# Loading query and key tiles singly instead of in neighbour-token groups, with more transposes by DMA, a new order and a longer warm-up

## The chip, the cores and the metric

The kernel runs on one core of a Trainium2 chip. The metric is the device time of one execution in microseconds, the median of three runs. The profiled span of the program, from its first to its last instruction, is a little shorter than that time.

## The reference, cut to what matters

Attention with a sliding window of 96 tokens and 8 global tokens, with a bias that falls with distance, is followed by an FFN that takes the elementwise maximum of three products (maxout) and multiplies it with an output matrix.

```python
batch, n_heads, seq, head_dim = (4, 8, 768, 64)       # q, k, v: float32
n_global, n_local = (8, 96)
n_tokens, d_model, d_ff = (3072, 512, 768)

def _attn_ref(q, k, v, n_global, n_local):
    scores = scale * np.matmul(q, k.transpose(0, 1, 3, 2))
    rel = pos[:, None] - pos[None, :]
    is_global = pos[None, :] < n_global
    is_local = (rel >= 0) & (rel < n_local)
    keep = is_global | is_local
    dist = np.where(is_global & ~is_local, float(n_local), np.abs(rel))
    slopes = 2.0 ** (-8.0 * (np.arange(H) + 1) / H)
    scores = np.where(keep, scores - slopes * dist, -1e9)   # shapes cut
    a = softmax(scores)                                     # written out in the original
    return np.matmul(a, v)

def _moe_ref(x, w1, w2, w3, w_out):
    h = np.maximum(np.maximum(x @ w1, x @ w2), x @ w3)
    return h @ w_out

# x is the attention's output with the heads side by side: (4 * 768, 512)
```

## The kernel before

The 3072 tokens are 24 tiles of 128. A tile attends to itself and the tile before it in its batch (six tiles a batch); the 8 global keys and values are copied over the first 8 rows of the tile before. Seven chunks of 4, 2, 2, 4, 4, 4 and 4 tiles then go through the FFN. Every step is a unit of a few instructions, and a string, `SCHEDULE`, says in which order the units are put into the program; each engine executes its own instructions in that order. A unit's last number often chooses the engine (0 ACT, 1 DVE, 2 POOL).

| unit | what it does |
|---|---|
| `l n.s` | load a part of a group of neighbouring tokens, q or k (L158) |
| `L T` | load q and k of tile T |
| `v T`, `w g.j`, `o i` | load v of tile T (L174), a part of w1, w2 or w3 (L417), a part of w_out |
| `c`, `C T.0`, `C T.1`, `W`, `Q` | cast a group's part, q and k of a tile, v of a tile, weights, w_out to bf16 |
| `x n.s`, `X T` | transpose q and k so that the head's 64 numbers lie in partitions |
| `S T.g` | scores of four heads and their exponential |
| `M T.g` | multiply by the mask with its bias (when the bias wasn't put in by matmul) |
| `A T` | attention times v, and division by the sum |
| `T T` | transpose the result for the FFN (xT) |
| `F c.f.j` | FFN: 128 columns of w1, w2 or w3 (j) for chunk c, and the maximum |
| `O c.t` | product with w_out of one tile, and its store; `E` is the last chunk's |
| `G`, `V` | global keys and values; `K`, `B` make mask and bias; `D` matmuls of zeros |

A group puts `e` neighbouring tokens of a head in one partition, so that a contiguous piece in memory is e × 256 bytes:

```python
GROUPS = [[0, 2], [2, 2], [4, 2], [6, 4], [10, 2]]       # first tile, tiles in the group
raw_pool  = ctx.enter_context(tc.tile_pool(name="raw", bufs=6))
rawv_pool = ctx.enter_context(tc.tile_pool(name="rawv", bufs=6))
stage_pool = ctx.enter_context(tc.tile_pool(name="stage", bufs=3))
psS = ...(bufs=1, PSUM)   # tags sp0 and sp1: scores, and attention's output
psH = ...(bufs=3, PSUM)   # FFN, output, some transposes
psT = ...(bufs=1, PSUM)   # transposes

def load_part(n, s):      # l: 512 KB in one DMA
    bb, t0, sz, a, j0, jn = part(n, s)
    ...
    src = (q, k)[a][bb, 2 * j0:2 * (j0 + jn), t0 * 128:(t0 + sz) * 128, :]
    nc.sync.dma_start(out=r, in_=src.rearrange("h (i e) d -> i h (e d)", e=sz))

def load(T):              # L: 256 KB for q, 256 KB for k
    ...
    for i, src in enumerate((q, k)):
        nc.sync.dma_start(out=r[:, i], in_=src[b, :, sl, :].rearrange("h s d -> s h d"))

def u_x(n, s, how):       # x: 8 transposes on TensorE, then copies to qkT on ACT, DVE or both
    ...
            for e in range(sz):
                for j in range(lo, hi):
                    nc.tensor.transpose(tp[:, e, j - lo], ..., identb)          # L239
    for (lo, hi, pool, tag, copy), tp in zip(halves, tps):
        copy(dst[:, lo:hi], tp.rearrange("c e j i -> c j i e"))                 # L243

def u_X(T, how):          # X: by DMA (how 4), or 8 transposes on TensorE
    ...
    if how == 4:
        nc.sync.dma_start_transpose(out=qk..., in_=qb[T]...)                    # L250
        return
    ...
    for a in range(2):
        for jp in range(NP):
            nc.tensor.transpose(tps[a][:, jp], qb[T][:, a, jp * 128:(jp + 1) * 128], identb)

def u_XT(T, how):         # T: by DMA (how 4, L340), or 4 transposes on TensorE
    ...
    for jp in range(NP):
        nc.tensor.transpose(tp[:, jp], x[:, jp * 128:(jp + 1) * 128], identb)   # L349
    copies[how](xT[c][:, :, i * 128:(i + 1) * 128], tp)

def u_F1(c, f, j):        # F
    ps = psH.tile([128, W], FP32, name="h", tag="h")
    for dm in range(4):
        nc.tensor.matmul(ps, w123[f // 2][:, dm, j, ...], xT[c][:, dm], ...)    # L361
    if j == 0:   nc.scalar.copy(h01, ps)                                        # L366
    elif j == 1: nc.vector.tensor_max(h01s[c, f], h01s[c, f], ps)               # L368
    else:        nc.vector.tensor_max(ht[c][:, f], h01s[c, f], ps)              # L370

def u_D(i, n):
    wp = psH.tile([128, 512], FP32, name="wp", tag="h")
    for _ in range(n):
        nc.tensor.matmul(wp, zeros[:, 0:128], zeros, start=True, stop=True)     # L436
```

`cast` can also split a tile between DVE (q) and POOL (k) when its last number is 3. All DMAs but one go through SyncE's queue, in the order of the program: one that waits for its data or its buffer holds up those behind it.

Of the kernel before, what the change touches and what calls it, by code (L numbers as in the profile page):

```python
# [22 lines left out]


SCHEDULE = """
    K0 K1 K2 K3 K4 K5 l1.0 l1.1 D0.3 c0.0.2 B0.1 B1.1 B2.1 B3.0 K6 B4.1 B5.1 c0.1.1 c1.0.2 x0.0.4 B6.1
    B7.1 x0.1.4 S0.0.1 v0 l2.0 l2.1 K7 S0.1.1 G0.0 S1.0.1 S1.1.0 x1.0.3 c1.1.2 M0.0 M0.1 M1.0 v1 x1.1.4
    C0.1.2 v2 A0.1 G1.2 S2.0.1 M1.1 c2.0.2 x2.0.1 C1.1.1 S2.1.0 G2.2 S3.0.1 M2.0 M2.1 C2.1.1 T0.1 S3.1.1
    M3.0 M3.1 c2.1.2 v3 A1.0 C3.1.0 w0.0 V1.2 x2.1.2 w1.0 A2.1 V2.2 A3.0 T1.0 T2.1 T3.1 W1.0.1 W0.0.0
    G3.2 S4.0.0 S4.1.0 F0.0.0 F0.1.0 M4.0 F0.2.0 F0.3.0 G4.1 S5.0.0 M4.1 S5.1.0 w0.1 W0.1.1 w0.2 W0.2.2  # L30
    V3.2 F0.0.1 F0.1.1 F0.0.2 F0.1.2 v4 C4.1.0 A4.0 V4.2 w1.1 W1.1.2 W2.0.0 F0.4.0 F0.5.0 M5.0 M5.1 w1.2
    W1.2.2 v5 W2.1.0 T4.0 F0.2.1 F0.3.1 l3.0 l3.2 F0.4.1 l3.1 c3.0.2 c3.2.2 F0.5.1 o2 C5.1.0 A5.1 l3.3
    F0.2.2 Q2.2 F0.3.2 W2.2.0 o0 T5.0 F0.4.2 o1 F0.5.2 x3.0.0 F1.0.0 F1.1.0 c3.1.1 F1.2.0 x3.2.0 Q0.2
    F1.0.1 F1.1.1 F1.2.1 l4.0 l4.1 c3.3.0 F1.0.2 F1.1.2 F1.2.2 x3.1.2 x3.3.1 F1.3.0 F1.4.0 Q1.2 F1.3.1
    S6.0.0 S6.1.0 v6 v7 v8 G6.0 F1.3.2 F1.5.0 v9 c4.0.1 F1.4.1 S7.0.0 S7.1.0 G7.2 v10 M6.0 M6.1 M7.0
    M7.1 O0.0.0 F1.4.2 c4.1.1 C6.1.2 C7.1.2 L12 F1.5.1 S8.0.0 S8.1.0 x4.0.0 O0.1.0 A6.0 x4.1.2 A7.1 V7.2
    F1.5.2 v11 T6.0 O0.2.0 T7.1 G8.2 C8.1.2 S9.0.0 S9.1.0 G9.1 v12 v13 O0.3.0 F2.0.0 F2.1.0 S10.0.0 M8.0
    M8.1 M9.0 M9.1 S10.1.0 C9.1.2 L13 L14 F2.0.1 F2.1.1 F2.0.2 A8.0 C12.0.1 F2.1.2 G10.2 O1.0.0 V8.2
    A9.1 X12.1 M10.0 M10.1 C10.1.0 C11.1.0 F2.2.0 S11.0.0 S11.1.0 M11.0 M11.1 L15 F2.3.0 F2.4.0 O1.1.0
    V9.2 A10.1 F2.2.1 V10.2 T8.0 F2.3.1 F2.5.0 T9.0 A11.1 F2.4.1 T10.0 F2.2.2 F2.3.2 T11.1 F2.4.2  # L40
    S12.0.0 S12.1.0 F2.5.1 C13.0.2 C14.0.2 C15.0.1 X13.4 F3.0.0 F3.1.0 F3.0.1 G12.1 C12.1.0 F3.2.0
    F3.1.1 F3.2.1 S13.0.0 S13.1.0 F2.5.2 v14 C13.1.0 C14.1.2 M12.0 M12.1 F3.0.2 F3.1.2 X14.4 F3.2.2
    X15.4 G13.2 M13.0 M13.1 S14.0.0 S14.1.0 F3.3.0 F3.4.0 F3.5.0 M14.0 M14.1 G14.1 A12.0 A13.1 F3.3.1
    F3.4.1 F3.5.1 S15.0.0 M15.0 S15.1.0 G15.0 v15 V13.2 L16 L17 v16 T12.4 v17 M15.1 O2.0.0 C15.1.0 A14.0
    V14.2 F3.3.2 F3.4.2 T13.4 F3.5.2 C16.1.0 C16.0.2 X16.3 T14.4 C17.0.2 A15.1 X17.4 O2.1.0 S16.0.0
    S16.1.0 G16.1 L18 V15.2 L19 T15.1 M16.0 O3.0.0 M16.1 F4.0.0 F4.1.0 F4.0.1 F4.1.1 C18.0.2 L20 C19.0.2
    A16.1 F4.2.0 F4.3.0 S17.0.0 S17.1.0 F4.2.1 F4.0.2 F4.3.1 v18 M17.0 v19 M17.1 X18.3 X19.4 C20.0.0
    V16.2 F4.1.2 C17.1.2 O3.1.1 A17.1 F4.2.2 F4.3.2 S18.0.0 M18.0 S18.1.0 M18.1 F4.4.0 T16.4 T17.4
    F4.4.1 C18.1.2 C19.1.1 F4.4.2 X20.4 G18.1 S19.0.0 S19.1.0 F4.5.0 L21 M19.0 M19.1 v20 F4.5.1 A18.0
    T18.4 F4.5.2 A19.1 T19.4 V19.1 C21.0.1 X21.4 G19.1 L22 C22.0.2 L23 X22.4 O3.2.1 O3.3.0 O4.0.1  # L50
    S20.0.0 S20.1.0 M20.0 G20.0 O4.1.0 F5.0.0 F5.1.0 F5.2.0 S21.0.0 S21.1.0 G21.2 F5.0.1 F5.1.1 M20.1
    M21.0 F5.3.0 F5.0.2 F5.1.2 F5.2.1 F5.2.2 v21 C20.1.1 C21.1.2 F5.4.0 S22.0.0 M21.1 S22.1.0 C23.0.0
    F5.3.1 M22.0 M22.1 F5.5.0 F5.3.2 A20.0 V20.2 G22.2 v22 F5.4.1 X23.4 v23 F5.5.1 T20.4 A21.1 V21.1
    T21.4 F5.4.2 F5.5.2 S23.0.0 S23.1.0 M23.0 O4.2.0 M23.1 C22.1.2 A22.0 C23.1.0 O4.3.0 V22.2 T22.4
    A23.1 T23.4 O5.0.1 O5.1.0 O5.2.1 O5.3.0 F6.0.0 F6.1.0 F6.0.1 F6.0.2 F6.2.0 F6.3.0 F6.4.0 F6.1.1
    F6.2.1 F6.1.2 F6.3.1 F6.4.1 F6.2.2 F6.3.2 F6.5.0 F6.4.2 F6.5.1 F6.5.2 E
"""


# [1 line left out]
def kernel(  # L61
# [13 lines left out]
    nc = tc.nc  # L75
# [12 lines left out]
    slopes = [2.0 ** (-8.0 * (h + 1) / H) for h in range(H)]  # L88
    sizes = [4, 2, 2, 4, 4, 4, 4]

    GROUPS = [[0, 2], [2, 2], [4, 2], [6, 4], [10, 2]]
    assert sum(sizes) == NTT
    chunks, where = [], {}
    for n in sizes:
# [27 lines left out]
    zeros = persist.tile([128, 512], BF16, name="zeros")  # L122
# [21 lines left out]
    def part(n, s):  # L144

        T0, sz = GROUPS[n]
        jn = {2: 4, 4: 2, 6: 1}[sz]
# [3 lines left out]
    def load_part(n, s):  # L151

        bb, t0, sz, a, j0, jn = part(n, s)
        r = raw_pool.tile([128, 2 * DM], FP32, name="rawp", tag="raw")
        r = r[:, 0:sz * jn * 128].rearrange("i (h x) -> i h x", h=2 * jn)
        raw["p", n, s] = r
        src = (q, k)[a][bb, 2 * j0:2 * (j0 + jn), t0 * 128:(t0 + sz) * 128, :]
        nc.sync.dma_start(out=r, in_=src.rearrange("h (i e) d -> i h (e d)", e=sz))  # L158
# [273 lines left out]
    def u_D(i, n):  # L432

        wp = psH.tile([128, 512], FP32, name="wp", tag="h")
        for _ in range(n):
            nc.tensor.matmul(wp, zeros[:, 0:128], zeros, start=True, stop=True)  # L436

    with tc.manual_schedule():
        load_part(0, 0)
        load_part(0, {2: 1, 4: 2, 6: 4}[GROUPS[0][1]])  # L440

# [68 lines left out]
```

The softmax here doesn't subtract the row's maximum and nothing guards it: scores larger than these inputs give would overflow.

## Time and profile before

The median is 180.43 us (180.39 to 180.48 in three runs).

| what | before |
|---|---|
| profiled span | 178.5 us |
| FFN matmuls, line L361 | 99.2 us busy |
| output matmuls, L376 | 33.1 us busy |
| score matmuls, L283 | 352 of them |
| transposes of groups, L239 | 96 of them, 8.5 us busy |
| transposes of xT, L349 | 52 of them, 4.9 us busy |
| transposes by DMA | 9 of q and k (median 3.3 us to landing), 11 of xT (2.4 us) |
| DMA packets | 83587, of which 66160 under 512 B |

In a page of the profile, the first part gives each engine's busy time, its share of the span and its instructions; PE is TensorE, PEld its weight loads, which run beside the matmuls. The second part cuts the span into 40 slices of 4.5 us; a digit is the busy share in tenths. The chain is followed back from the last instruction to what released each step. Line numbers are those of the kernel before and are marked in the code above. `tpp` is a group's transposed q or k in PSUM, `tp` that of a single tile, `xtp` the transposed result of attention, `sp` scores, `op` attention's output, `h` the FFN's.

### The profile page before, as it was taken

The page shows a single profiled execution, that of the slowest core. Times are in us where ns is not written, and L with a number is a line of the kernel's source. Part 1 is how long each engine was busy: PE and PEld are TensorE (multiplying, and loading weights), DVE is VectorE, ACT ScalarE, POOL GpSimd, SP SyncE. Part 2 cuts the span into 40 slices and gives each one's busy share as a digit, 9 for nine tenths or more (in the row PEclk, how much of TensorE's full clock was granted, in tenths as well). Part 3 has the DMA queues.
Part 4 walks back from the last instruction along what each step waited for, and adds up shares of the span by engine and source line. Part 5 has one row for each costly group of instructions (what it writes and reads, how often), then busy time and mean ns, then how long its engine had stood idle before and what let it go on. Part 6 is the DMA issues. An engine that isn't in the chain of part 4 may idle for free.

```text
span 178.5 us, 3963 instructions
## 1 busy us (share of the span) xinstructions
PE 167.1 (94%) x1529; PEld 95.9 (54%) x1551; DVE 119.1 (67%) x237; ACT 103.2 (58%) x160; POOL 37.4 (21%) x65
## 2 busy tenths in 40 slices
PE   3599799999999999999999999999999999999991
PEld 0455645458866677845555555454454555444451
DVE  4519975977796689748978448978358986137610
ACT  4867898646689958555753936351862543440131
POOL 4255203543343012210006024100020401000000
PEclk9999999999999999999999999999999999999998
DMA  5999999999998899899544999988989664700015
GB/s 139 292 270 243 357 321 383 319 361 356 252 194 229 218 254 227 142 204 234 92 90 122 167 253 231 145 172 152 182 156 300 123 129 147 252 12 4 0 47 190
DMA packets 83587, 35.52 MB, mean 199 GB/s; under 512 B 66160, under 2 KB 78320, under 8 KB 83568
## 3 DMA queue, kind: packets, MB, share of 16 engines
q1 hardware_dynamic: 83424, 35.20, 83.6%
q8 instruction: 12, 0.20, 0.5%
q10 hardware_dynamic: 144, 0.07, 0.1%
q14 instruction: 7, 0.06, 0.1%
HBM read 25.17 MB, written 6.29 MB: 176 GB/s over the span
## 4 chain that ended last, share of the span: by engine, by line
PE 88%; ACT 3%; DVE 2%; POOL 2%; issue 1%; DMA 1%; POOLq 0%; ACTq 0%
PE h L361 53%; PE po L376 16%; PE sp L283 7%; PE op L322 3%; PE op L325 3%; PE tpp L239 3%; PE xtp L349 2%; ACT wmask L300 2%; PE sp L275 2%; DMA out_dram<-ost 1%; DVE qkT L243 1%; DVE xb L332 1%; ACT ost L382 1%; ACT P L288 1%; PE tp L261 1%
## 5 line engine op out<-in xcount | busy, mean ns | idle before, releaser
L361 PE MATMUL h<-xT,w 128*128 128x512 bf16 (+1 forms) x491 | 99.2, 348 | 0.7 <-issue 0.2
L361 PEld LDWEIGHTS <-w 128*128 128x128 bf16 x504 | 47.0, 98 | 40.4 <-ACT w L427 0.2
L288 ACT ACTIVATE P<-sp 128x1024 bf16<-128x1024 f32 (+1 forms) x48 | 43.4, 954 | 20.4 <-PE sp L283 20.2
L368 DVE TENSOR_TENSOR h<-h,h 128x512 bf16<-128x512 bf16 (+1 forms) x42 | 25.2, 609 | 25.6 <-PE h L361 15.5
L366 ACT CAST h<-h 128x512 bf16<-128x512 f32 (+1 forms) x42 | 21.6, 532 | 21.5 <-PE h L361 21.3
L376 PE MATMUL po<-wo,ht 128*128 128x512 bf16 (+2 forms) x147 | 33.1, 362 | 0.5
L370 DVE TENSOR_TENSOR ht<-h,h 128x512 bf16<-128x512 bf16 (+1 forms) x42 | 25.0, 606 | 3.7 <-PE h L361 3.0
L307 DVE TENSOR_TENSOR P<-P,wmask 128x1024 bf16<-128x1024 bf16 x36 | 24.8, 716 | 3.6 <-ACT P L288 3.5
L382 ACT COPY ost<-po 128x512 f32<-128x512 f32 (+2 forms) x20 | 11.2, 564 | 18.4 <-PE po L376 11.2
L376 PEld LDWEIGHTS <-ht 128*128 128x128 bf16 x156 | 14.0, 98 | 13.8
L332 DVE TENSOR_TENSOR xb<-op,rz 128x512 bf16<-128x512 f32 x24 | 16.6, 691 | 0.8
L283 PEld LDWEIGHTS <-qkT 64*128 64x128 bf16 x352 | 10.2, 96 | 10.0 <-issue 8.0
L283 PE MATMUL sp<-qkT 64*128 64x128 bf16 x352 | 15.2, 223 | 0.4 <-DVE xb L332 0.4
L322 PEld LDWEIGHTS <-P 128*128 128x128 bf16 x192 | 12.5, 97 | 2.7 <-ACT P L288 0.2
L221 POOL COPY va<-vaf 8x260 int32<-8x260 int32 x14 | 6.3, 449 | 34.7 <-PE op L325 34.7
L198 POOL CAST qkb<-raw 128x1024 bf16<-128x1024 f32 x7 | 7.2, 1037 | 27.6 <-DMA raw<-in_k_dram 27.6
L322 PE MATMUL op<-va,P 128*128 128x65 bf16 x160 | 12.4, 193 | 0.3 <-ACT va L189 0.2
L239 PE MATMUL tpp<-identb,qkp 128*128 128x128 bf16 x96 | 8.5, 246 | 4.0 <-POOL qkp L183 3.5
L325 PEld LDWEIGHTS <-P 128*128 128x128 bf16 x160 | 10.4, 97 | 1.8 <-issue 0.2
L239 PEld LDWEIGHTS <-qkp 128*128 128x128 bf16 x96 | 7.0, 112 | 5.8 <-POOL qkp L183 4.4
L325 PE MATMUL op<-va,P 128*128 128x65 bf16 x128 | 9.9, 193 | 0.1
L243 ACT COPY qkT<-tpp 128x1024 bf16<-128x1024 bf16 (+1 forms) x9 | 7.9, 873 | 3.4 <-PE tpp L239 3.4
(66 smaller groups left out, 107.7 us busy)
## 6 DMA issues: line engine op xcount, KB each, us to landing
rawv<-in_v_dram SPq DMA_DIRECT2D x24, 256.0 KB, 4.9
out_dram<-ost SPq DMA_DIRECT2D x23, 256.0 KB, 2.3
rawp<-in_q_dram SPq DMA_DIRECT2D x6, 512.0 KB, 7.3
rawp<-in_k_dram SPq DMA_DIRECT2D x6, 512.0 KB, 7.7
wst<-in_moe_w_dram SPq DMA_DIRECT2D x3, 1024.0 KB, 10.3
raw<-in_q_dram SPq DMA_DIRECT2D x12, 256.0 KB, 4.2
raw<-in_k_dram SPq DMA_DIRECT2D x12, 256.0 KB, 4.7
wst<-in_moe_w_dram SPq DMA_DIRECT2D x3, 512.0 KB, 8.6
```

The costliest lines, as they stand in the source:

```text
L239: nc.tensor.transpose(tp[:, e, j - lo], qb["p", n, s][:, e, 2 * j:2 * j + 2].rearrange("i h d -> i (h d)"), identb)
L283: nc.tensor.matmul(sp[:, hh, j2, ds], qT(T - ds, 1)[hsl, jp], qT(T, 0)[hsl, jp], start=not how, stop=True, skip_group_check=True)
L288: nc.scalar.activation(P[:, :, 0:n], sp.rearrange("p a b d n -> p (a b) d n")[:, :, 0:n], AF.Exp, bias=0.0, scale=scale)
L307: nc.vector.tensor_mul(P, P, wmask[:, g, :, 0:2])
L322: nc.tensor.matmul(o, P[:, i, 0], heads(va[T])[:, h], start=True, stop=(t == 0), skip_group_check=True)
L325: nc.tensor.matmul(o, P[:, i, 1], heads(va[T - 1])[:, h], start=False, stop=True, skip_group_check=True)
L332: nc.vector.tensor_tensor(out=x.rearrange("p (g h) d -> p g h d", g=2), in0=o4[:, :, :, 0:64], in1=rz[:, :, :, None].to_broadcast([128, 2, ...
L361: nc.tensor.matmul(ps, w123[f // 2][:, dm, j, (f % 2) * 128:(f % 2) * 128 + 128], xT[c][:, dm], start=(dm == 0), stop=(dm == 3))
L366: nc.scalar.copy(h01, ps)
L368: nc.vector.tensor_max(h01s[c, f], h01s[c, f], ps)
L370: nc.vector.tensor_max(ht[c][:, f], h01s[c, f], ps)
L376: nc.tensor.matmul(po, ht[c][:, f, tt * 128:(tt + 1) * 128], wo[:, f, cols], start=(f == 0), stop=(f == NF - 1))
```

## The change

Only the tiles 0 to 3 are still loaded as groups of neighbouring tokens. The tiles 4 to 23 are loaded singly, in pieces of 256 bytes. Of these 20 tiles 13 are transposed by DMA, seven by TensorE; 14 of the 24 results of attention are transposed by DMA. The matmuls of zeros are shorter (128 columns in place of 512), and 54 of them in place of 3 stand at the start, so as to keep TensorE active until data comes; three more stand further on. The order of all units is new, and many casts and copies go to other engines: 10 instead of 5 of the outputs are copied by DVE, 9 instead of 4 of the values cast by DVE.

```diff
 SCHEDULE = """
-    K0 K1 K2 K3 K4 K5 l1.0 l1.1 D0.3 c0.0.2 B0.1 B1.1 B2.1 B3.0 K6 B4.1 B5.1 c0.1.1 c1.0.2 x0.0.4 B6.1
-    B7.1 x0.1.4 S0.0.1 v0 l2.0 l2.1 K7 S0.1.1 G0.0 S1.0.1 S1.1.0 x1.0.3 c1.1.2 M0.0 M0.1 M1.0 v1 x1.1.4
-    C0.1.2 v2 A0.1 G1.2 S2.0.1 M1.1 c2.0.2 x2.0.1 C1.1.1 S2.1.0 G2.2 S3.0.1 M2.0 M2.1 C2.1.1 T0.1 S3.1.1
-    M3.0 M3.1 c2.1.2 v3 A1.0 C3.1.0 w0.0 V1.2 x2.1.2 w1.0 A2.1 V2.2 A3.0 T1.0 T2.1 T3.1 W1.0.1 W0.0.0
-    G3.2 S4.0.0 S4.1.0 F0.0.0 F0.1.0 M4.0 F0.2.0 F0.3.0 G4.1 S5.0.0 M4.1 S5.1.0 w0.1 W0.1.1 w0.2 W0.2.2
-    V3.2 F0.0.1 F0.1.1 F0.0.2 F0.1.2 v4 C4.1.0 A4.0 V4.2 w1.1 W1.1.2 W2.0.0 F0.4.0 F0.5.0 M5.0 M5.1 w1.2
...                                                  (21 more lines of the old order)
+    D0.54 B0.1 B3.0 l1.1 l1.0 c1.0.2 B4.1 B6.1 B7.1 K3 K7 B2.1 c0.1.1 K1 K6 c0.0.0 x0.0.0 B1.1 x0.1.3 K5
+    K2 c1.1.1 S1.0.1 M1.0 B5.1 S0.1.1 x1.1.3 M0.1 S0.0.1 M0.0 G0.2 v0 C0.1.1 K4 S1.1.0 x1.0.3 G1.1 A0.0
+    S2.1.0 S2.0.1 G2.2 v1 C1.1.1 v3 T0.0 C3.1.2 M1.1 A1.1 L4 C4.0.3 M2.1 v2 C2.1.1 S3.0.1 V1.2 S3.1.1
+    G3.1 A2.0 V2.0 L5 C5.0.2 w0.0 X4.0 A3.1 T2.1 T1.0 D3.3 K0 W0.0.1 X5.0 T3.1 M2.0 S4.1.0 w0.1 W0.1.2
+    S4.0.0 G4.2 F0.0.0 F0.1.0 w0.2 W0.2.1 M4.0 F0.0.1 F0.1.1 M3.0 F0.0.2 F0.1.2 M4.1 w1.0 W2.0.0 S5.1.0
+    W1.0.2 S5.0.0 F0.4.0 F0.5.0 v4 M5.1 M5.0 V3.2 C4.1.2 A4.1 F0.2.0 F0.3.0 T4.0 w1.1 W2.1.1 V4.1
+    W1.1.1 v5 C5.1.1 F0.4.1 F0.3.1 A5.1 F0.5.1 w1.2 F0.2.1 T5.1 W2.2.2 F0.5.2 L6 C6.0.2 W1.2.0 F0.4.2
+    F0.2.2 L7 X6.0 v6 F1.0.0 F1.4.0 F0.3.2 S6.0.0 S6.1.0 F1.4.1 F1.4.2 C6.1.1 C7.0.2 F1.1.0 F1.1.1
+    F1.1.2 M6.0 F1.3.0 M6.1 F1.5.0 F1.5.1 o0 L8 X7.4 F1.2.0 G6.2 F1.3.1 A6.1 F1.5.2 C8.0.2 v7 X8.3
+    F1.0.1 S7.1.0 S7.0.0 Q0.1 G7.2 F1.2.1 F1.0.2 F1.2.2 T6.1 o1 F1.3.2 o2 Q2.1 S8.0.0 Q1.2 C7.1.2 L9 L10
+    C10.0.2 M7.1 v8 v9 L11 M7.0 C9.1.2 S8.1.0 G8.0 C9.0.1 X10.4 v10 M8.0 O0.2.1 L12 v11 L13 v13 O0.0.0
...                                                  (18 more lines of the new order)
@@
-    GROUPS = [[0, 2], [2, 2], [4, 2], [6, 4], [10, 2]]
+    GROUPS = [[0, 2], [2, 2]]
@@ def u_D(i, n):
-            nc.tensor.matmul(wp, zeros[:, 0:128], zeros, start=True, stop=True)
+            nc.tensor.matmul(wp[:, 0:128], zeros[:, 0:128], zeros[:, 0:128], start=True, stop=True)
```

More of the change, by code (lines that the diff above doesn't have):

```diff
@@ L31 @@
-    V3.2 F0.0.1 F0.1.1 F0.0.2 F0.1.2 v4 C4.1.0 A4.0 V4.2 w1.1 W1.1.2 W2.0.0 F0.4.0 F0.5.0 M5.0 M5.1 w1.2
[L32 to L55, printed above, removed]
@@ L56 @@
-    F6.2.1 F6.1.2 F6.3.1 F6.4.1 F6.2.2 F6.3.2 F6.5.0 F6.4.2 F6.5.1 F6.5.2 E
+    D0.54 B0.1 B3.0 l1.1 l1.0 c1.0.2 B4.1 B6.1 B7.1 K3 K7 B2.1 c0.1.1 K1 K6 c0.0.0 x0.0.0 B1.1 x0.1.3 K5
[3 more added lines that the diff above has]
+    S4.0.0 G4.2 F0.0.0 F0.1.0 w0.2 W0.2.1 M4.0 F0.0.1 F0.1.1 M3.0 F0.0.2 F0.1.2 M4.1 w1.0 W2.0.0 S5.1.0
@@ new lines @@
+    C10.0.2 M7.1 v8 v9 L11 M7.0 C9.1.2 S8.1.0 G8.0 C9.0.1 X10.4 v10 M8.0 O0.2.1 L12 v11 L13 v13 O0.0.0
+    A7.0 V7.0 X9.0 O0.1.1 S9.1.0 S9.0.0 T7.1 M8.1 O0.3.0 C8.1.2 M9.0 C11.0.2 F2.0.0 G9.1 M9.1 F2.4.0
+    A8.0 F2.3.0 F2.3.1 V8.0 F2.0.1 A9.0 X11.3 T8.4 F2.1.0 V9.2 S10.1.0 S10.0.0 F2.1.1 F2.1.2 F2.0.2
+    G10.2 C10.1.2 M10.1 C12.0.3 F2.2.0 T9.4 F2.5.0 M10.0 C13.0.2 X13.4 L14 S11.1.0 M11.1 S11.0.0 F2.2.1
+    O1.0.1 v12 X12.3 A10.1 G12.1 v14 L15 C11.1.0 F2.2.2 O1.1.0 M11.0 C14.0.2 V10.1 T10.1 X14.4 F2.3.2
@@ new lines @@
+    A11.0 L16 F2.5.1 C15.0.2 X15.4 F2.4.1 F2.4.2 v15 S12.0.0 S12.1.0 T11.1 F2.5.2 O2.1.0 M12.1 M12.0
+    C13.1.1 F3.0.0 C14.1.2 S13.0.0 S13.1.0 G13.2 M13.1 M13.0 F3.2.0 C12.1.1 F3.4.0 F3.3.0 F3.4.1 F3.3.1
+    F3.3.2 A13.0 A12.1 T12.4 T13.4 V13.1 F3.0.1 F3.4.2 F3.0.2 S14.1.0 M14.1 S14.0.0 G14.2 F3.1.0
+    F3.1.1 F3.1.2 M14.0 S15.1.0 M3.1 L17 v16 C16.0.3 M15.1 C15.1.2 X16.4 S15.0.0 O2.0.0 G15.2 M15.0
+    F3.5.0 F3.2.1 A14.1 T14.4 V14.2 F3.2.2 A15.0 T15.4 V15.2 L19 L18 C18.0.2 F3.5.1 F3.5.2 O3.0.1 v18
@@ new lines @@
+    S16.1.0 M16.1 S16.0.0 G16.2 M16.0 C19.0.1 O3.1.0 F4.0.0 C16.1.0 F4.4.0 F4.4.1 C17.0.0 X17.4 F4.1.0
+    F4.3.0 A16.0 F4.1.1 F4.1.2 F4.3.1 F4.2.0 X18.4 C18.1.1 F4.0.1 S17.1.0 S17.0.0 F4.0.2 F4.2.1 M17.0
+    S18.1.0 M18.1 S18.0.0 X19.4 L20 v17 v20 M18.0 F4.4.2 F4.2.2 v19 S19.0.0 S19.1.0 C20.0.2 X20.4 M17.1
+    M19.0 T16.4 C17.1.2 O3.2.0 L21 C21.0.2 V16.0 A18.0 F4.5.0 M19.1 G18.1 T18.4 F4.3.2 A17.0 C19.1.0
+    F4.5.1 F4.5.2 A19.1 T17.4 G19.1 T19.4 O3.3.1 S20.0.0 S20.1.0 M20.0 X21.4 C20.1.2 v22 L22 v21 O4.3.0
@@ new lines @@
+    M20.1 O4.1.0 L23 C22.1.2 G20.1 F5.0.0 V19.1 A20.1 C22.0.2 F5.2.0 F5.5.0 F5.3.0 X22.4 S21.0.0 S21.1.0
+    M21.0 v23 C21.1.2 C23.0.0 X23.4 F5.3.1 F5.3.2 M21.1 O4.2.1 V20.2 F5.2.1 F5.2.2 F5.0.1 F5.0.2 A21.1
+    V21.1 C23.1.1 G21.2 F5.1.0 F5.1.1 S22.0.0 M22.0 S22.1.0 G22.1 M22.1 F5.4.0 F5.4.1 F5.1.2 F5.4.2
+    S23.0.0 M23.0 S23.1.0 M23.1 T20.4 F5.5.1 O4.0.0 T21.4 A22.0 T22.4 F5.5.2 V22.0 A23.1 T23.4 O5.3.1
+    O5.1.1 O5.0.1 O5.2.1 F6.0.0 F6.4.0 F6.5.0 F6.4.1 F6.4.2 F6.2.0 F6.0.1 F6.0.2 F6.2.1 F6.2.2 F6.5.1
@@ L57 @@
+    F6.1.0 F6.1.1 F6.3.0 F6.3.1 F6.3.2 F6.1.2 F6.5.2 E
 """
```

## The prediction, made before the changed kernel was timed

> **What bounds the kernel now.** I read the page first: the shares of busy time, the 40 slices and the chain that ended last.
>
> ```profile
> span 178.5 us, 3963 instructions
> ...
> PE 167.1 (94%) x1529; PEld 95.9 (54%) x1551; DVE 119.1 (67%) x237; ACT 103.2 (58%) x160; POOL 37.4 (21%) x65
> ...
> PE   3599799999999999999999999999999999999991
> ...
> DMA  5999999999998899899544999988989664700015
> ...
> PE 88%; ACT 3%; DVE 2%; POOL 2%; issue 1%; DMA 1%; POOLq 0%; ACTq 0%
> ```
>
> TensorE is 94% busy and carries 88% of the chain. Only the first five slices (some 22 us) and the last are short of nine. The DMA row is full for two thirds of the span as well: a second resource with little to spare.
>
> Matmuls are pipelined, so busy time alone proves little. I took the starts of all matmuls and their usual distance when nothing waits: 216 ns at 512 columns, 109 at 256, 56 at 128 columns (transposes too), 29 to 30 for the 65-column ones, about 34 for a score matmul (two run side by side). After the first FFN matmul, extra distances of over 100 ns sum to only about 6 us, almost all single ones of 0.1 to 0.2 us with no engine named as the cause. So from there on the time is TensorE's work at full speed. The windows say the same:
>
> ```profile
> 0.00:10.00 10.00, 4.80 (x29) 2.43 (x31) 5.33 (x23) 6.46 (x14) 4.28 (x14) 1.00 0.91 222
> 10.00:20.00 10.00, 9.54 (x134) 6.13 (x135) 6.67 (x12) 7.74 (x12) 4.45 (x7) 1.00 1.24 270
> ...
> 100.00:110.00 10.00, 9.84 (x80) 5.11 (x80) 5.33 (x10) 5.78 (x9) 2.98 (x4) 1.00 1.12 243
> ```
>
> Columns: stretch, length, then PE, PE weight load, DVE, ACT and POOL busy (with counts), clock, DMA share, GB/s. PE is busy in 10 to 20 us too, but weighting its matmuls by the distances above gives 6.6 us of full-speed work there and 2.2 us in the first ten. The chain tells why:
>
> ```profile
> 7.69 1.01 PE tpp L239 x8
> ...
> 12.25 0.98 PE tpp L239 x8
> 13.26 1.82 DVE qkT L243 x2
> ...
> 21.61 0.70 DVE xb L332
> ...
> 22.35 0.40 PE xtp L349 x4
> 22.75 0.55 PE sp L283 x16
> 23.30 0.34 PE h L361
> ...
> 41.04 0.45 PE tpp L239 x8
> ```
>
> Eight transposes take 1.01 and 0.98 us at 7.7 and 12.3 us, and 0.45 us at 41 us: TensorE starts at half speed. The trace's clock record begins 13.5 us into the span, at full clock, so the page's clock row shows nines for a stretch that it doesn't know. The first FFN matmul (L361) starts at 23.30 us.
>
> **What the Trainium skill says.** "TensorE: Matmul & The Clock Gate", Part 1, states that the array is held at half clock until it has been active for a window of some 3.4 us, and that short 128-column matmuls go from about 107 to 56 ns. The trace agrees on the two speeds (1.01 us / 8 = 126 ns with the latency of the last, against 56 ns); the release came only at 13.5 us because three zero matmuls end at 2.7 us and TensorE then sits idle until 6.2 us. The same page, Part 4, adds that transposes do not count as activity in the same way; this trace fits, as most early work is transposes, but does not prove it. "DMA: Bandwidth & Descriptors", "Specifications", says that transfers under 512 B fall short of line rate. The packet records agree: a packet of 256 B takes 21.7 ns (11.8 B/ns), 512 B 33.2 ns (15.4 B/ns), 1 KB 52.6 ns (19.5 B/ns).
>
> **The change, part by part.**
>
> *Transposes leave TensorE.* Before, 120 transposes of q and k run on TensorE: 96 for grouped tiles (L239) and 24 for tiles 12, 16 and 18. After, the two groups need 32, and tiles 4, 5, 6, 8, 9, 11 and 12 need 8 each: 88. On the xT side 13 tiles used TensorE with 4 each (52); after, 10 tiles, 40. So 32 + 12 = 44 go, × 56 ns = 2.46 us. All 44 are gone from the part after the first FFN matmul: both orders have the same list ahead of it (scores of tiles 0 to 4, attention and xT of 0 to 3, 48 transposes for tiles 0 to 5). In a saturated stage every one of them counts. Scores, attention, FFN and output matmuls are the same number. Gain 2.5 us.
>
> *54 short matmuls of zeros at the start.* Cold, at 107 ns, they would last 5.8 us, from 1.2 to 7.0 us; if the clock rises on the way they end near 6. The first q part lands at 5.04 us, is cast on ACT after five short preparations (about 7.0 us), so they hold up nothing. From about 5 us TensorE is at full speed. The TensorE part of the chain from 7.69 to 13.26 us (5.6 us of cold work) shrinks to about 2.8 us. But this isn't gained in full. What comes next is a ladder of score, exponential (1.03 us each on ACT), mask (0.68 us), attention, normalising (0.2 + 0.7 us) for four tiles, sharing two PSUM score buffers. Stepping it through with these durations, I find the last normalised tile about 20.6 us (before: 22.3), and its transpose about 21.3.
>
> *Loads and weights.* The first FFN matmul also needs w1's first part, which lands at 21.23 us before. Ahead of it lie 4.25 MB in both orders (before: six parts and four v; after: four parts, tiles 4 and 5, four v). Two tiles now come as 1 MB of 256 B pieces: before, 256 KB of those land every 1.15 us and a 512 KB part every 1.8 us, so 4 × 1.15 against 2 × 1.8: 1 us later. But the two v that before were held back (issued at 10 to 13 us) go out at once, so I keep 21.2 to 22. The cast on DVE takes 0.69 us. First FFN matmul: about 22.4, a gain of 0.9 us. The last part of w3, which the first chunk's end needs, lands at 34.2 before. Adding the steps of 1.1 (v), 1.5 (512 KB of weights) and 2.9 (1 MB) in the new order I get 35.1 to 36; TensorE has 14 FFN groups × 0.86 us + 2 us of attention to do before it needs it, that is until 36.6. Just in time.
>
> *More DMA.* Tiles 4 to 11: 16384 packets × 21.7 ns against 4096 × 33.2 + 2048 × 52.6, over 16 engines: 22.2 − 15.2 = 7 us. Transposes by DMA: 4 more of q/k (1024 packets each) and 3 more of xT (512): 5632 × 21.7 / 16 = 7.6 us. Total 150 to about 165 us of engine time in a span whose last 20 us need little. Nearly all of it lies beside TensorE, as tiles came 11 to 20 us before their scores in the old order. It gets thin at 36 to 60 us: stepping through, w_out's last part lands near 50 and its first use is near 51; tile 10's v and k and tile 8's v lie within 1 to 2 us of need. I allow 0.8 us for stalls in all.
>
> *Copies and casts move.* Outputs copied by DVE 5 to 10 (+3 us), two casts of w and two of w_out more on DVE (2.8 us), value casts 4 to 9 (2.1 us), and the global rows of v from POOL to DVE and ACT. DVE has 36 busy of 50 us at 100 to 150 us; some 8 us more over the whole span does not make it the bound, but a PSUM buffer of the FFN (three of them) can be freed later. Included in the 0.8.
>
> Sum: 180.43 − 2.46 − 0.9 + 0.8 = 177.9 us.
>
> **The rivals.** (a) Loads become the bound at 35 to 60 us. For it: the DMA row at nine there, 7 us of extra packets just then, and one in-order SP queue in which a DMA transpose waits for its cast while loads stand behind it. Against: before, the weights and tiles came early, and the new order puts a tile's load one or two tiles farther ahead. It would cost 2 to 4 us: 179.5 to 182. (b) The clock gain is hidden or lost: either the ladder on ACT and DVE keeps its 23.3 us, or the clock falls back between 6 and 10 us as only transposes run. For it: 9.37 us of 10 busy on ACT at 20 to 30 us. Then only the transposes count: 178.8. (c) The start comes out better, as the old chain to 13.3 us was all cold TensorE and weights also come sooner: first FFN matmul at 21.5 and no stalls, 176.2. (d) DVE becomes the engine that frees PSUM too late: many small stalls, 1 to 3 us. DVE's 67% speaks against, its long queues of mask, normalise and maximum for it.
>
> **Range and chances.** The 2.5 us of transposes are the firm part; the start is worth 0 to 2, stalls cost 0 to 4. Expected 177.9 us, 8 times in 10 from 175.3 to 181.3. Faster by over 2% means under 176.8, which needs (c) or nearly no stalls: 0.34. Slower by over 2% means above 184.0: 0.06. Within 2%: 0.60.
>
> **What would show it.** Right: eight early transposes in about 0.45 us by 8 us, first L361 near 22.4, tp groups of 88 and xtp of 40, the last matmul about 2.5 us earlier relative to the first FFN matmul, TensorE without gaps of over 0.3 us after 25 us. Wrong: PE stalls at L361 or L376 released by a cast of w or w_out or by DMA at 35 to 60 us; first L361 still at 23 us; early transposes at over 100 ns; idle before L361 that ends with a DVE or ACT read of h.

## The result, and the profile after

The changed kernel takes 187.17 us (median of four runs, 186.36 to 188.8) against 180.43: a ratio of 1.0385, with a 95% interval of 1.0338 to 1.0432. It is slower, and outside the predicted range.

The page of the changed kernel, with the lines that answer to those shown of before:

```profile
span 185.1 us, 3990 instructions
...
PE   7778998999999699899799799999899999999992
...
DMA  5999999989999999999999999999899963710005
DMA packets 99811, 36.96 MB, mean 200 GB/s; under 512 B 88528, under 2 KB 94544, under 8 KB 99792
...
PE 49%; DMA 22%; SPq 19%; issue 4%; DVE 2%; POOL 1%; ACT 1%; ACTq 0%; POOLq 0%; DVEq 0%
```

Three things are to be seen. The PE row starts higher (7, 7 for 3, 5 in the first two slices): the zeros. It then has single eights, sevens and a six up to slice 29, where before it was solid nines. And the DMA row stays at eight or nine up to slice 32, where before it fell to 4 and 5 in the middle. The chain says the same in another way: TensorE falls from 88% of it to 49%, and DMA with the queue that issues it (SPq) rises from 1% to 41%.

I split the span with the starts of the matmuls. TensorE's own work is counted: the instructions of the program after the first FFN matmul, times their usual distances of the prediction, which are the same in both traces (medians 216, 109 and 56 ns). The waits are what is left.

| part of the span, us | before | after | difference |
|---|---|---|---|
| up to the first FFN matmul | 23.27 | 24.29 | +1.02 |
| from there to the last matmul | 151.36 | 156.96 | +5.60 |
| of this, TensorE's own work, counted | 149.03 | 146.57 | −2.46 |
| of this, waits: the rest | 2.33 | 10.39 | +8.06 |

1.02 − 2.46 + 8.06 = 6.6 us, which is the whole of 185.1 − 178.5. So the change takes 2.46 us of work from TensorE, by count, and adds 8 us of waits. Waits of over 0.3 us after 25 us sum to 7.9 us (before: 0.34). The prediction's "about 6 us" of extra distances before were for the most part no waits: the trace of before lacks 13 of the 504 FFN matmuls and 9 of the 156 of the output, and each missing one looks like 216 ns more, 4.8 us in all.

Two stretches of the windows, in which the columns are those of the prediction's windows; first the kernel before, then the changed one:

```profile
24.30:75.00 50.70, 50.38 (x556) 34.67 (x561) 39.86 (x78) 37.37 (x60) 16.21 (x23) 1.00 1.05 272
75.00:150.00 75.00, 74.26 (x642) 38.48 (x653) 54.38 (x103) 40.68 (x60) 11.92 (x19) 1.00 0.84 168
```

```profile
24.30:75.00 50.70, 47.80 (x496) 31.68 (x503) 41.29 (x83) 30.44 (x49) 15.97 (x22) 1.00 1.07 248
75.00:150.00 75.00, 70.36 (x593) 35.69 (x602) 53.71 (x101) 36.51 (x52) 14.85 (x22) 1.00 1.07 212
```

In the first stretch the DMA share hardly differs (1.05, 1.07), but it moves 248 instead of 272 GB/s: the same packet time carries less. In the second the share goes from 0.84 to 1.07. The times of packets overlap, so a share can pass 1 and is no share of a fixed capacity. SyncE's issues say it more plainly: from 75 to 150 us SyncE was issuing, or held in an issue, for 49.9 us before and for 64.9 of the 75 us after. The old stream had slack from 75 us on; the new one has hardly any.

What the waits wait for is in the chain of the changed kernel (start, length, what):

```profile
19.38 10.61 DMA wst<-in_moe_w_dram
...
31.12 1.90 PE h L361 x8
...
56.65 4.80 DMA rawv<-in_v_dram
...
63.58 0.19 PE op L322
...
98.93 5.93 DMA qkT<-qkb
...
104.91 0.62 PE sp L283 x16
```

A part of the weights lands at 29.99 us (27.05 before) and holds the FFN, once ACT has cast it, at 31.12 us (1.10 us). A value tile lands at 61.45 us, POOL casts, and attention starts at 63.58 after a wait of 1.83 us, the largest. A DMA transpose takes 5.93 us and holds scores at 104.91 us (1.35 us); one of tile 14 costs 0.75 us at 91 us, with 0.51 more until POOL has copied the global keys; another costs 0.33 at 137 us. A wait of 1.06 us of the FFN at 132.9 us is put down to a copy on DVE, but a DMA transpose of xT landed 0.25 us before its end, and in E6, E11 and E12 below the wait at this place is put down to such a landing. One of 0.98 at 77.2 (a copy on ACT whose output buffer had to be stored first) completes the list of the large ones. Weights, values, transposes and stores are all a little late; what they share is the stream of transfers.

The lead shows it too: the time from a tile's k landing to its first score matmul.

| lead, us | tile 12 | 13 | 14 | 15 |
|---|---|---|---|---|
| before | 16.4 | 12.2 | 13.8 | 17.6 |
| after | 7.6 | 6.6 | 7.6 | 5.5 |

In a lead, a tile is cast, put through SyncE's queue and transposed (4.2 us median to landing) before its scores. For tiles 8 and 9 it is 5.5 and 3.0 us. A short lead alone makes no wait, though: in the kernel before, tiles 18, 19, 21, 22 and 23 had only 8.9, 9.8, 6.9, 6.4 and 10.8 us, and no wait of over 0.3 us came there, with a DMA share of 0.86 from 112 to 145 us (1.06 in the same stretch after).

### The profile page after: what moved, and what is told of

The parts are those of the page before. It is cut to its first block, busy times and chain, and to the rows that moved or that the text cites. A ratio compares the mean times of both kernels' runs of the same rounds, so it can differ in the third digit from the quotient of the medians.

```text
span 185.1 us, 3990 instructions
## 1 busy us (share of the span) xinstructions
PE 168.4 (91%) x1541; PEld 97.0 (52%) x1561; DVE 127.7 (69%) x253; ACT 93.0 (50%) x141; POOL 37.1 (20%) x62
## 2 busy tenths in 40 slices
DMA packets 99811, 36.96 MB, mean 200 GB/s; under 512 B 88528, under 2 KB 94544, under 8 KB 99792
## 4 chain that ended last, share of the span: by engine, by line
PE 49%; DMA 22%; SPq 19%; issue 4%; DVE 2%; POOL 1%; ACT 1%; ACTq 0%; POOLq 0%; DVEq 0%
PE h L361 32%; PE po L376 9%; SPq L167 8%; DMA qkT<-qkb 8%; DMA wst<-in_moe_w_dram 6%; SPq L174 6%; DMA out_dram<-ost 4%; PE sp L283 3%; DMA rawv<-in_v_dram 3%; DMA raw<-in_k_dram 2%; SPq L158 2%; PE op L322 2%; PE op L325 1%; POOL va L189 1%; SPq L417 1%
## 5 line engine op out<-in xcount | busy, mean ns | idle before, releaser
L307 DVE TENSOR_TENSOR P<-P,wmask 128x1024 bf16<-128x1024 bf16 x36 | 28.0, 788 | 13.4 <-ACT P L288 13.2
L368 DVE TENSOR_TENSOR h<-h,h 128x512 bf16<-128x512 bf16 (+1 forms) x42 | 25.3, 606 | 11.1 <-PE h L361 9.7
L198 POOL CAST qkb<-raw 128x1024 bf16<-128x1024 f32 x13 | 13.9, 1069 | 59.9 <-DMA raw<-in_k_dram 57.0
L376 PEld LDWEIGHTS <-ht 128*128 128x128 bf16 x156 | 14.2, 98 | 14.5 <-DVE ht L370 0.5
L283 PEld LDWEIGHTS <-qkT 64*128 64x128 bf16 x352 | 10.1, 96 | 14.5 <-issue 6.6
L322 PE MATMUL op<-va,P 128*128 128x65 bf16 x160 | 12.9, 196 | 2.0 <-POOL va L189 1.7
L382 ACT COPY ost<-po 128x512 f32<-128x512 f32 (+2 forms) x15 | 8.2, 553 | 12.7 <-PE po L376 8.7
L322 PEld LDWEIGHTS <-P 128*128 128x128 bf16 x192 | 12.9, 99 | 3.2 <-ACT wmask L300 0.7
L325 PEld LDWEIGHTS <-P 128*128 128x128 bf16 x160 | 10.8, 99 | 3.4 <-issue 1.8
L382 DVE COPY ost<-po 128x512 f32<-128x512 f32 (+1 forms) x11 | 7.2, 652 | 7.1 <-PE po L376 7.1
L189 POOL CAST va<-rawv 128x512 bf16<-128x512 f32 x12 | 9.3, 778 | 9.0 <-DMA rawv<-in_v_dram 9.0
L325 PE MATMUL op<-va,P 128*128 128x65 bf16 x128 | 9.9, 193 | 0.1
L331 DVE RECIPROCAL rz<-op 128x8 f32<-128x8 f32 x24 | 4.8, 202 | 6.2 <-PE op L325 6.1
L436 PE MATMUL wp<-zeros 128*128 128x128 bf16 x57 | 5.4, 281 | 1.2 <-DVE tiny L443 1.2
```

Source lines behind the costliest of these rows:

```text
L283: nc.tensor.matmul(sp[:, hh, j2, ds], qT(T - ds, 1)[hsl, jp], qT(T, 0)[hsl, jp], start=not how, stop=True, skip_group_check=True)
L307: nc.vector.tensor_mul(P, P, wmask[:, g, :, 0:2])
L322: nc.tensor.matmul(o, P[:, i, 0], heads(va[T])[:, h], start=True, stop=(t == 0), skip_group_check=True)
L325: nc.tensor.matmul(o, P[:, i, 1], heads(va[T - 1])[:, h], start=False, stop=True, skip_group_check=True)
L376: nc.tensor.matmul(po, ht[c][:, f, tt * 128:(tt + 1) * 128], wo[:, f, cols], start=(f == 0), stop=(f == NF - 1))
L382: copy(ost, po)
```

## The experiments

Three theories stood at the start. P (packets): loads and DMA transposes in 256-byte packets fill the DMA engines, so all transfers come late. Q (queue): SyncE's one in-order queue is the cause, as a DMA transpose that waits for its cast holds up the loads behind it. O (order): the new order and the new engines of casts and copies make TensorE wait, whatever the loads. A fourth question was whether the start, with its zeros, gains anything.

**E1: the changed kernel, with pieces of 512 bytes.** Single q and k loads keep their bytes and places in the order, but take two neighbouring tokens of half of the heads, so the tile gets other tokens: only the time is to be read.

```diff
+        s0 = min(t * 128, S - 256)
-        nc.sync.dma_start(out=r[:, i], in_=src[b, :, sl, :].rearrange("h s d -> s h d"))
+        nc.sync.dma_start(out=r[:, i]...,      # same tile, seen as 4 x 128 numbers a partition
+                          in_=src[b, 0:4, s0:s0 + 256, :].rearrange("h (i e) d -> i h (e d)", e=2))
```

> The changed kernel with the same order, but the single loads of q and k fetch the same bytes in pieces of 512 B instead of 256 B (they fetch other tokens, so the output is not the reference's). Theory P (small pieces: too many packets delay the loads, and TensorE waits for them): 20480 packets fewer, about 14 us less DMA time; the waits of TensorE after 30 us mostly go, 180 to 182 us. Theory Q (the queue is in order, and loads stand behind transposes and stores that wait): little changes, 185 to 187.5 us. Theory O (the order and the choice of engines themselves stall TensorE): 185 to 187.5 us.

180.1 us (20 runs, 178.97 to 181.6), ratio 0.9985 (0.9966 to 1.0004): 7.1 us of the changed kernel's time gone. Lines of its page:

```profile
PE   7666999999999999999999999999899999999991
...
DMA  4999999999999999999778599999899704700015
DMA packets 79331, 36.96 MB, mean 207 GB/s; under 512 B 47568, under 2 KB 74064, under 8 KB 79312
...
PE 69%; DVE 14%; DMA 10%; issue 3%; ACT 1%; SPq 1%; POOL 0%; ACTq 0%; DVEq 0%; POOLq 0%
```

The same bytes (36.96 MB) in 20480 packets fewer, and the DMA row has slack again in slices 20 to 23. SPq falls from 19% of the chain to 1%. The leads of tiles 12 to 15 are back at 12.0, 10.9, 12.2 and 10.1 us, the waits after the first FFN matmul at 4.49 us. From 75 to 150 us SyncE is issuing for 53.7 us instead of 64.9. Order, transposes and casts are those of the changed kernel, so P holds for the loads (whether their packets fill the DMA engines or SyncE's time to issue stays open), and what Q and O do without small packets can be only a small part. The rest tells something too: with the packets gone the kernel is no faster than before, because 2.2 us more of waits are left (4.49 − 2.33), and they eat the 2.46 us of transposes. E1 takes away more than the change had added: 12288 of its 20480 packets are of tiles 12 to 23, which were in pieces of 256 bytes before too. E5 below takes only the tiles that the change cut up.

**E2: the kernel before, with its group loads in 256-byte pieces** (of other heads' numbers; again only the time counts).

```diff
-        nc.sync.dma_start(out=r, in_=src.rearrange("h (i e) d -> i h (e d)", e=sz))
+        m = min(8 * bb + 2 * j0, B * H - 16)                     # 16 rows of (b h), one tile of tokens
+        nc.sync.dma_start(out=r..., in_=...[m:m + 16, t0 * 128:(t0 + 1) * 128, :].rearrange("m i d -> i m d"))
```

> The kernel before with its own order and its own 12 group loads, but each group load fetches its 512 KB in pieces of 256 B (of other heads, so the output is not the reference's). Theory P: about 7 us of packets more before 60 us and 4 more before 12 us; the loads of tiles 4 to 11 and the weights come 2 to 6 us later, 183 to 187 us. Theories Q and O: at most 1 us, 180.4 to 181.5 us.

184.86 us, ratio 1.024 (1.0225 to 1.0256). Its page:

```profile
PE   3396869999999999999999999999999999999992
...
DMA packets 97923, 35.52 MB, mean 194 GB/s; under 512 B 90736, under 2 KB 92656, under 8 KB 97904
```

Nearly as many packets as after, and yet the PE row is solid nines from slice 7 on. The first FFN matmul comes at 27.44 us, 4.2 later than before: w1's first part lands at 24.88 us (21.23 before). After it the waits are 2.5 us, as before. The leads (12.8, 10.8, 12.4, 15.9 us) are those of the old order and of a TensorE that started later. Part of the late start is E2's own, as it also cuts up the tiles 0 to 3, which the change left in groups. So packets alone don't make TensorE stumble in the middle of this order; whether that is the order or the late start, E2 by itself doesn't tell. E11 below does.

**E3: the kernel before, with the 54 zeros.**

```diff
-    ... D0.3 c0.0.2 ...
+    ... D0.54 c0.0.2 ...        (and 128 columns instead of 512)
```

> The kernel before with only the 54 short matmuls of zeros in place of the 3 long ones. TensorE at full clock from some 5 us on. If the first FFN matmul hangs on the cold chain from 7.7 to 13.3 us: 1 to 1.5 us less, 179 to 179.5 us. If ACT's and DVE's ladder or the landing of the first weights holds it: 180.0 to 180.5 us.

180.74 us (20 runs), ratio 1.0016 (1.0006 to 1.0025). The clock record is full from 6.5 us, and the first FFN matmul comes at 23.30 us instead of 23.27. Its chain says why:

```profile
10.08 7.67 DMA rawv<-in_v_dram
...
17.78 0.44 DVE va L189
```

A value tile lands at 17.75 us, and attention waits for it. A TensorE that is at full clock 7 us sooner arrives sooner at the same wait. The zeros are worth nothing here; the time even lies just above the second of the two expectations.

**E4: the changed kernel, with values loaded through ACT's queue,** to take them out of the queue in which transposes wait.

```diff
-        nc.sync.dma_start(out=r, in_=v[b, :, sl, :].rearrange("h s d -> s h d"))
+        nc.scalar.dma_start(out=r, in_=v[b, :, sl, :].rearrange("h s d -> s h d"))
```

> The changed kernel with the 24 loads of v issued by ACT's queue instead of SyncE's, so that they stand behind no transpose or store and there are two queues. Theory Q: 2 to 4 us less, 183 to 185 us. Theory P: the same packets, so no gain: 186 to 189 us, as ACT also pays for issuing.

217.06 us, ratio 1.2001 (1.1977 to 1.2026). It failed as a test of Q. Lines of ACT's timeline:

```profile
21.17 1.02 ACT L288 ACTIVATE P<-sp 128x1024 bf16<-128x1024 f32 x1 [7.47 <-PE sp L283]
...
23.06 1.01 ACTq L174 DMA_DIRECT2D rawv<-in_v_dram  x2
```

ACT issues a load when it has come to it in its own work: the first v goes out at 11.78 us instead of 4.85, later ones behind exponentials that themselves wait for scores. Attention waits 14.1 us in all for values cast by DVE, 9.1 in one piece. The Trainium skill ("DMA: Bandwidth & Descriptors", "Issuing engines are not separate DMA queues") says that another issuing engine saves only issue time, as the 16 DMA engines are shared. This run can't tell whether that holds here, for it paid another price: the loads lost their run-ahead, and the first FFN matmul came at 44.1 us. Q was not isolated by it.

**E5 and E6: 512-byte pieces for a part of the tiles only:** 4 to 11 in E5, 12 to 23 in E6.

```diff
+            if T < 12:              # E6: T >= 12
+                (the load of E1)
+            else:
                 (the load as changed)
```

> The changed kernel, where only the tiles 4 to 11, those that the change took out of the groups, fetch q and k in pieces of 512 B (of other tokens, so the output is not the reference's); tiles 12 to 23 stay at 256 B. 8192 packets fewer, about 5.8 us less DMA time. If it is these tiles' small pieces: the waits at 31 and 63 us and the late start (24.3 us) go, 182 to 183.5 us. If instead the whole stream of loads and transposes up to the last tile is too long, whatever its place: about 5.8 us less waiting, 181.5 to 182.5 us. If these tiles don't matter: 186.5 us or more.

> The complement: tiles 4 to 11 at 256 B as in the changed kernel, tiles 12 to 23 in pieces of 512 B, though they were already at 256 B before the change. 12288 packets fewer, about 8.7 us less DMA time. If the damage is done by tiles 4 to 11 alone: at most 1 us, 186 to 187 us. If the whole stream is too long: the waits after 75 us (some 5 us) go, 181.5 to 183 us, with those at 31 and 63 us left.

E5: 182.11 us, ratio 1.0096 (1.006 to 1.0132); the waits at 31 and 63 us are gone, but not the late start (24.91 us). These are the tiles that the change cut into smaller pieces, so 5.06 of the 6.74 us that it lost hang on them. E6: 183.54 us, ratio 1.0177 (1.016 to 1.0194); it keeps waits at 61.7, 64.8 and 77.3 us (0.74, 0.82, 1.07), and 151.36 us from before become 153.38. So the early tiles cost more (5.06 us for 8192 packets) than the late ones (3.63 us for 12288), but the loss is not confined to one stage. A stream that has caught up early has lead left later: in E5 the tiles 12 to 15, still in 256-byte pieces, have leads of 12.6, 11.1, 11.0 and 8.5 us, against 7.6, 6.6, 7.6 and 5.5. So the two runs may remove some of the same waits. Their sum of 8.7 us against the 7.1 of E1 fits that but doesn't show it, as the four runs of the changed kernel spread over 2.4 us.

**E7 and E9: the changed kernel, with seven DMA transposes back on TensorE** (X of tiles 7, 10, 16, 18; T of 8, 9, 15).

```diff
-    X7.4  X10.4  X16.4  X18.4  T8.4  T9.4  T15.4
+    X7.3  X10.3  X16.3  X18.3  T8.1  T9.0  T15.1       E9: each X also moved to just ahead of its scores
```

> The changed kernel with the extra DMA transposes undone: q and k of tiles 7, 10, 16 and 18 and the results of tiles 8, 9 and 15 are transposed by TensorE, as many as before. 5632 packets fewer, 7.6 us less DMA time; 44 transposes more, 2.5 us more TensorE work. If the whole stream is too long: 4 to 5 us of waiting less, in sum 184 to 186 us. If only the loads' pieces matter: 2.5 us more, 189 to 190 us.

> As the run that undid the extra DMA transposes, but q and k of tiles 7, 10, 16 and 18 are transposed by TensorE just ahead of their own scores, not where the DMA transpose stood, so that TensorE's in-order queue doesn't meet a load that hasn't landed. 5632 packets fewer, 2.5 us more TensorE work. If the whole stream of small packets is too long, transposes included: 4 to 5 us of waiting less than in the changed kernel, 184.5 to 186 us. If the DMA transposes cost nothing: 189 to 190 us.

E7: 192.55 us, ratio 1.0679 (1.0658 to 1.07). A DMA transpose stands early in the order so that its latency is hidden; a transpose on TensorE in that place stops TensorE's own queue until k is cast: 4.54 us at 58.0 us, 1.90 at 101. That is more than either expectation, and not a fair trial, so E9 moved them. E9: 189.22 us, ratio 1.0481 (1.0447 to 1.0515). TensorE's work is 149.03 us again, and the waits are 10.44 us, as with DMA transposes (10.39), but of another kind, as this line of its waits shows:

```profile
PE sp L283 <- DVE qkT L264: 3.9, 4, 2.2
```

Now scores wait for DVE's copy of the transpose that TensorE has just made. The time falls where it was expected "if the DMA transposes cost nothing". But E9 removes their packets and adds a copy at the last moment, so it stays inconclusive on what seven DMA transposes cost.

**E8 and E10: the kernel before, with more DMA transposes:** X12, X18, T8 and T9 in E8, X12 and X18 alone in E10.

```diff
-    X12.1  X18.3  T8.0  T9.0
+    X12.4  X18.4  T8.4  T9.4            E10: the two X only
```

> The kernel before, with q and k of tiles 12 and 18 and the results of tiles 8 and 9 transposed by DMA, in the stretch where its DMA engines are idle for much of the time (85 to 100 us). 24 transposes of 56 ns fewer: 1.3 us less, 179.0 to 179.4 us, if the old order has the room; 180.4 or more if the transposes come too late and TensorE waits for them.

> The kernel before, with only q and k of tiles 12 and 18 transposed by DMA, of the four changes of the earlier run; the results of tiles 8 and 9, whose FFN follows at once, stay on TensorE. 16 transposes fewer, 0.9 us less TensorE work: 179.5 us if the wait of 2.4 us in the earlier run came from the two results alone; 181 us or more if the transposes of q and k bring waits too.

E8: 183.37 us, ratio 1.0173 (1.0117 to 1.0228). Most of the loss in its trace (182.53 us, the others up to 184.55) is one wait, as TensorE's timeline shows (idle time and releaser in brackets):

```profile
77.57 1.67 PE L361 MATMUL h<-xT,w 128*128 128x512 bf16 x6 [2.19 <-DMA xT<-xb]
```

The FFN of tiles 8 to 11 follows their attention closely, so a DMA transpose of xT just ahead of it lies open. E10 leaves these on TensorE: 180.49 us, ratio 1.0003 (0.9995 to 1.0011), where 16 transposes × 56 ns = 0.9 us were to be had. That lies between its two expectations. In the trace, of the slowest of 13 runs, 0.45 us were gained from the first FFN matmul on (150.91 for 151.36), which came 0.6 us later; the order up to there is the same, so that part is scatter. It was the attempt at a version that beats both kernels, and it only equals the kernel before.

**E11: the changed kernel, with 3 zeros instead of 54.**

```diff
-    D0.54 B0.1 ...
+    D0.3 B0.1 ...
```

> The changed kernel with 3 instead of 54 matmuls of zeros at the start. If the first weights and the loads' stream hold the start: the same within 0.5 us of the changed kernel, 186.5 to 187.7 us. If the 54 were worth what the prediction gave them: 1 us or more slower, 188 us or more.

187.26 us, ratio 1.0388 (1.0367 to 1.0408): the same as with them.

```profile
PE   1576989989999999999999989999699999999992
```

The PE row starts at 1, 5, 7 instead of 7, 7, 7, and the first FFN matmul comes 2.8 us later (27.12 us). But the waits of over 0.3 us after it fall from 7.9 to 4.2 us, and the end is where it was. A TensorE that starts 2.8 us earlier only waits longer for the same transfers: the last DMA transpose lands at 160.49 us without the zeros and at 160.06 with them. So the transfers set the end here, not the time at which TensorE starts.

E11 also answers what E2 left open. The two have nearly as many packets (99811 and 97923) and reach the first FFN matmul at nearly the same time (27.12 and 27.44 us), but from there on the new order waits for 7.6 us and the old one for 2.5. So the new order, with its seven more DMA transposes, has its part in the loss. It isn't the lead of the loads alone: E11's tiles 12 to 15 have 11.8, 10.3, 11.3 and 8.7 us, not far below E2's but for tile 15, and its largest wait, 1.64 us at 133 us, is for a DMA transpose of xT.

**E12: the changed kernel, with each of the 13 DMA transposes doing q only;** k's half is set to zero by POOL, so the k of these tiles is left out (the score matmuls still run).

```diff
-            nc.sync.dma_start_transpose(out=qk.rearrange("p a j s -> p (a j) s"), in_=qb[T]...)
+            nc.sync.dma_start_transpose(out=qk[:, 0], in_=qb[T][:, 0])
+            nc.gpsimd.memset(qk[:, 1], 0.0)
```

> The changed kernel, in which the 13 DMA transposes of q and k do only q; k is set to zero by POOL instead (so the output is not the reference's). Everything else stays, TensorE's work too. 6656 packets fewer, 9.0 us less DMA time, and POOL has 13 short memsets more. If the whole stream of 256 B packets sets the pace, transposes like loads: 4 to 5.5 us less than the changed kernel, 181.7 to 183.2 us. If only the loads count, because a transpose comes late and little waits for it: at most 1.5 us less, 185.7 us or more.

184.52 us, ratio 1.0238 (1.021 to 1.0266): 2.65 us less than the changed kernel, between the two expectations.

The scores' waits for DMA transposes are gone. A wait for a value's cast at 62 us stays (1.17 us), and at 79 us scores wait 1.70 us for DVE's normalising, which itself waited until a DMA transpose of xT landed, 6.1 us after its issue, and freed a buffer. The four runs that took packets away from the changed kernel and left TensorE's work as it was:

| run | packets fewer | us less | us per 1000 |
|---|---|---|---|
| E5: loads of tiles 4 to 11 | 8192 | 5.06 | 0.62 |
| E6: loads of tiles 12 to 23 | 12288 | 3.63 | 0.30 |
| E1: both | 20480 | 7.07 | 0.35 |
| E12: half of the q/k transposes | 6656 | 2.65 | 0.40 |

The changed kernel's own runs spread over 2.4 us, so these are rough. Within that, a transpose's packets cost about what a load's do. A transpose of half the size landed hardly sooner (median 4.0 us for 4.2), so the gain hardly comes from the shorter transfer itself.

## Why the prediction was wrong

*Transposes, −2.46 us: right, as far as it goes.* 44 transposes left TensorE after the first FFN matmul (108 before, 64 after), at a median distance of 56 ns in both traces. That is a count; as TensorE no longer sets the pace alone, it did not come off the time.

*The start, −0.9 us: wrong, +1.02.* The zeros did what was said: their distance falls from 107 to 56 ns at 5.2 us. But w1's first part landed at 22.65 us and not at 21.2 to 22, and the ladder ahead of it wasn't shortened as stepped: the last normalised tile was ready at 22.97 us, not at about 20.6. (What lies ahead of w1 is 4.19 MB in both orders, not 4.25, which changes nothing.) Rival (b) had it: "the ladder on ACT and DVE keeps its 23.3 us". E3 shows it in the old order, 23.30 against 23.27, with a load of v as the reason. E11 shows what the prediction missed: with three zeros the new order reaches the first FFN matmul at 27.12 us, 3.9 later than the old one with its three. The prediction took the two starts for alike; the zeros made good 2.8 us of a slower start. And E11 shows that these 2.8 us don't reach the end.

*DMA time, "150 to about 165 us": nearly right.* The packets' time is 167.7 us over 16 engines (150.5 before). The sum is good to some 5 us only: the same packets as before took 145.4 us in E3, the same as after 174.2 in E11. What failed is the sentence after it: *"Nearly all of it lies beside TensorE"*, and with it the term *"0.8 us for stalls in all"*: the waits grew by 8.06 us. I set 165 us of transfers against a span of 180 and took the rest as slack. But the last DMA transpose lands 25.1 us before the end in both kernels (at 153.33 and 160.06 us), so the stream has to be done some 25 us before the end: predicted, by 151 us. Up to the last transpose the windows give a DMA share of 0.94 before and 1.01 after. That left no room for 15 us more. Two cautions: the last transpose lands some 25 us before the end in every run here, so this doesn't tell which of the two sets the pace (E11 does); and a share of about 1 is not yet a loss, since E1 has 1.01 up to its last transpose, with 160 us of packets, and is as fast as the kernel before.

*The argument beside it was wrong too.* "Tiles came 11 to 20 us before their scores" held for the tiles 12 to 17 and 20 of the old order (12.2 to 19.2 us), not for the other five loaded singly (6.4 to 10.8), and for none but 17 of the new one (14.6). Rival (a)'s "against", that the new order puts a load farther ahead, is refuted by the leads of 5.5 to 7.6 us of tiles 12 to 15: places in an order are not time when the queue ahead is full. My stepping was 1 to 4 us early throughout: the last w3 part landed at 37.77 us (35.1 to 36), w_out's last at 53.5 (near 50).

*Rival (a) had the mechanism, not the size or place.* "Loads become the bound at 35 to 60 us", for 2 to 4 us. It is 8 us, at 31 and 63 us but also at 91, 105 and 133: E6 shows 3.6 us from tiles 12 and up. Both parts count, the packets and the new order: E1 takes away packets and the loss is gone; E2 has nearly as many in the old order and waits for 2.5 us where E11, which starts as late, waits for 7.6. Rival (d), DVE freeing PSUM late, does not appear among the larger waits.

*Left open:* how the loss divides between packets and order, and what in the order it is (lead, transposes, engines of casts), whether the DMA engines or SyncE's issuing of many small pieces is what limits the stream, the exact share of the transposes (E7 and E9 were confounded, E12 rests on four runs), and head-of-line waiting in SyncE's queue (E4 was no test). E1 leaves that last one little room.

## What to carry to other kernels

When a change moves work from a full engine to the DMA, sum the packets' time and compare it with the time up to the last transfer that something needs, not with the whole span; if they are close, don't count what is added as free. The sum alone doesn't tell what it will cost: here 17 us more of packets' time (150.5 to 167.7) came with 8 us of waits, and E1's 9 us more with 2. Measure the lead of each load (landing to first use) in the trace before, and step it anew for the new order. A faster start was worth nothing while a stream of transfers set the end (2.8 us in E11); try it alone before adding it to a sum.

## What the runs showed of the hardware

**Small pieces also hold the issuing queue.** A line of the timeline of SyncE's queue in the changed kernel (start, length of the issue):

```profile
12.39 2.41 SPq L174 DMA_DIRECT2D rawv<-in_v_dram  x1
```

256 KB in 256-byte pieces held SyncE for 2.4 us here; a load of q of the same size took 0.42 us at 40.97 us. With 512-byte pieces the median issue of a q or k load falls from 0.88 us to 0.57 (E1). That an issue lasts until earlier packets have made room, and that SPq's 19% of the chain is the full stream seen from the other side, is my reading and not shown: three other transfers were in flight at 40.97 us too. In 12 to 14.5 us the DMA moved 222 GB/s with 256-byte pieces; in the old order 290 GB/s at 12 to 14 us with larger ones. The Trainium skill ("Perfetto Trace Analysis", 'What "DMA-bound" means') names the DMA engines and the issuing sequencer as separate bounds, with larger descriptors as the answer to both. E1 agrees that larger pieces relieve both: with 512-byte pieces DMA goes from 22% to 10% of the chain and SPq from 19% to 1%.

**The clock fell back with TensorE in use.** Two windows of the changed kernel, and the second of them in E1:

```profile
12.00:15.30 3.30, 1.63 (x26) 1.03 (x26) 3.27 (x8) 2.48 (x4) 0.00 (x0) 1.00 1.31 219
15.30:18.70 3.40, 3.40 (x38) 2.04 (x38) 1.58 (x5) 1.77 (x3) 1.73 (x4) 0.52 0.82 180
```

```profile
15.30:18.70 3.40, 3.10 (x42) 1.54 (x42) 2.45 (x6) 2.37 (x4) 1.91 (x4) 1.00 0.88 216
```

After 3.3 us in which TensorE was half busy, with no gap of over 0.7 us, the clock was 0.52 for 3.4 us. The Trainium skill ("TensorE: Matmul & The Clock Gate", "HAM oscillation — how this bites in real kernels") warns of gaps of over 3.4 us; here there was none, so such gaps alone don't tell it. E1, as busy in the 3.3 us ahead (1.63 us, though with 35 matmuls for 26), kept its clock; why the two differ is open. It isn't what made the kernel slow: another run of it with a mean clock of 0.996 instead of 0.991 took 187.41 us.
